# Batch 0 of a Fourier mixing and gated FFN kernel stored in the layout of the other batches

## The chip, the cores and the metric

One of the eight cores of a Trainium2 chip runs the whole program. The metric is the device time of one execution in microseconds (us); the figure before is the median of three runs. A profiled execution stands beside them, and every duration in this text comes from it. A core has TensorE (PE in the profile; its weight loads are PEld), VectorE (DVE), ScalarE (ACT), GpSimd (POOL) and SyncE (SP), which here issues nearly all DMAs. Each engine works through its own instructions in order, and semaphores hold an instruction back until its inputs are there.

## What is computed

```python
def _attn_ref(x):                      # x: (8, 3008, 256) float32
    X = np.fft.fft(x, axis=1)
    X = np.fft.fft(X, axis=2)
    return X.real.astype(np.float32)

def _moe_ref(x, w_gate, w_val, w_out): # x: (24064, 256); 256x1536, 256x1536, 1536x256
    gate = 1.0 / (1.0 + np.exp(-(x @ w_gate)))
    val = x @ w_val
    return (gate * val @ w_out).astype(np.float32)
```

The second function is applied to the first one's result, flattened to 24064 rows. The three weight arrays come as float64 and are converted on the chip.

## The kernel before

**The transform.** S is 3008 rows, M = S/2 = 1504, D = 256. The real part of the transform along the rows needs a cosine sum `pk` of one half of the features and a sine sum `qk` of the other. Rows s, S-s, M+s and M-s are given together as four "h" planes; folding them (additions and subtractions of planes) leaves sums over s = 0..752 for even k and for odd k (`blk` 0 and 1), with the tables `stab` of cosines and sines. The transform along the features is folded too, and its matrix `dt` is multiplied into the gate and value weights beforehand (`merge`, tiles `ps`, copied to `G`). The feature at position D/2 has a row of its own, E, which enters through `ge` and `EK`: `seed` writes E times `ge` into a gate tile's PSUM bank before the products are added to it.

**The loop.** Per batch there are six chunks of k (252 columns, the last 246) and twelve tiles of 128 hidden units, 576 iterations in all. Iteration i does `front_a(i)` (products of `pk` into the PSUM tile `pf`), `gate_a(i-1)` (a sigmoid into h, and z = ae - pf on VectorE), `part(i)` (a ScalarE copy `ae` of the half-finished `pf`, two buffers), `seed(i+1)`, `gate_b(i-1)` (h times pf; a sigmoid; h times z; then sums of h on GpSimd, tile `sf`), `back` (five of fifteen products of a group of three tiles with the output weights, tile `po`, five iterations after the group's first tile) and `front_b(i)` (products of `qk`). Work that is due once stands in a dictionary `side` by iteration. Sums of `po` on VectorE (`c`), transposes and stores wait in the list `later`; two or three are done at the end of each iteration. `NFT`, called `i0` there, is 12. The group of iterations 3p, 3p+1, 3p+2 is called group p.

**Batches 1 to 7** take their x from a DRAM copy `XR` that `mirror_x` lays out: partitions 0 to 63 hold even s, 64 to 127 odd s, and positions 3 to 5 hold the rows 752-s. `fold_ops` folds them on GpSimd, spread over the iterations before; `whole` then does the sums of one `blk` with pairs of matmuls over 63 rows each (`both`). All sums of batch 1 stand in iteration 64 (`g0`); those of a later batch stand 40 iterations into the batch before it. For odd k these batches turn x by tangents on VectorE (`TURN`) and use a table that `table_odd` prepares on GpSimd.

**Batch 0 and the opening.** Batch 0's x and table lie row s = 6p+q on partition p, q in 0..5 (126 partitions), and are loaded in thirds of q. Eight weight tiles of 256 columns (`weight_load`, jobs 0 to 7) come first on SP, then thirds of x and of the cosine table in turn, the sine table, and jobs 8 to 13. A conversion is two ScalarE passes (`weight_parts`), three VectorE passes and one GpSimd addition (`weight_join`); then TensorE merges. `ge_sums` makes `ge` of a merged tile with products of one column. After all eight, VectorE folds the thirds (`third`, `feats`), each followed on TensorE by the E products (`e0_sums`) and the cosine sums of that third (`sums`, 126 rows). `e0_copies`, `e0_row` and `e0_spread` build E's row and its chunk; `then` and `places` combine even and odd sums into `pk`. The sine sums follow, between the first `front_a`. Twelve warming products (`warm`) run before the first weight is there.

E of batches 1 to 7 is folded on GpSimd at iteration 36 (`e_fold`), multiplied at iteration 40 (`e_sums`, 126 rows) and combined on VectorE. At iteration 42 `table_again` loads the table once more, in the other batches' layout. `e_rows` loads a chunk of E's row into `EK`, eleven iterations ahead.

## Time and profile before

| | us |
|---|---|
| median of three runs | 1928.14 (1926.18 to 1929.38) |
| the profiled execution | 1926.51 |
| its span | 1924.7 |
| TensorE busy | 1915.4 |
| VectorE busy | 1430.8 |
| ScalarE busy | 1346.6 |
| GpSimd busy | 1563.8 |

The page divides the span into 40 slices; a digit is the busy share of a slice in tenths. "Busy" for TensorE runs from a matmul's start to a modelled end, so it hides short gaps; starts in the timeline are the surer reading. A float32 matmul appears as two records. In the timeline's lines the columns are the start in us, the length of the run of equal instructions, engine, line, operation, out<-in, shapes and count; in brackets stands the idle time before it and what ended it. A line of the matmuls is always L135, so they are told apart by tile.

Two groups of the table of costliest work are of use beside the lines below: GpSimd's additions of 128 columns by 384 take 1.014 us (L452) and those of 512 columns 1.289 (L436); VectorE's product of 252 columns takes 0.405 (L702).

### The profile page before, as it was taken

The page shows a single profiled execution, that of the slowest core. Times are in us where ns is not written, and L with a number is a line of the kernel's source. Part 1 is how long each engine was busy: PE and PEld are TensorE (multiplying, and loading weights), DVE is VectorE, ACT ScalarE, POOL GpSimd, SP SyncE. Part 2 cuts the span into 40 slices and gives each one's busy share as a digit, 9 for nine tenths or more (in the row PEclk, how much of TensorE's full clock was granted, in tenths as well). Part 3 has the DMA queues.
Part 4 walks back from the last instruction along what each step waited for, and adds up shares of the span by engine and source line. Part 5 has one row for each costly group of instructions (what it writes and reads, how often), then busy time and mean ns, then how long its engine had stood idle before and what let it go on. Part 6 is the DMA issues. An engine that isn't in the chain of part 4 may idle for free.

```text
span 1924.7 us, 34460 instructions
## 1 busy us (share of the span) xinstructions
PE 1915.4 (100%) x11260; PEld 1787.2 (93%) x11260; DVE 1430.8 (74%) x3210; ACT 1346.6 (70%) x3147; POOL 1563.8 (81%) x2806
## 2 busy tenths in 40 slices
PE   9999999999999999999999999999999999999999
PEld 6899989999999999999999999999999999999998
DVE  7747887787777877777777777777777777777776
ACT  5877667767777677776777767777677767777775
POOL 3499989978898788986888878888788986777775
PEclk9999999999999999999999999999999999999999
DMA  9451422211131211202112121121200100011101
GB/s 305 135 87 38 106 80 56 52 58 37 20 76 27 80 17 29 76 14 80 25 46 51 20 81 21 47 50 25 80 14 15 26 17 14 15 22 20 26 17 30
DMA packets 167403, 97.89 MB, mean 51 GB/s; under 512 B 128602, under 2 KB 157372, under 8 KB 165432
## 3 DMA queue, kind: packets, MB, share of 16 engines
q1 hardware_dynamic: 166670, 95.17, 20.6%
q8 instruction: 91, 1.49, 0.3%
q14 instruction: 88, 0.72, 0.1%
q10 hardware_dynamic: 522, 0.50, 0.1%
q0 software_dynamic: 32, 0.00, 0.0%
HBM read 70.40 MB, written 47.24 MB: 61 GB/s over the span
## 4 chain that ended last, share of the span: by engine, by line
PE 94%; DMA 3%; DVE 1%; ACT 0%; SPq 0%; issue 0%; ACTq 0%; DVEq 0%
PE pf L135 49%; PE po L135 40%; PE ev L135 2%; DMA st<-in_stab_dram 2%; PE rows L135 1%; PE od L135 1%; DMA xr<-in_xf_dram 1%; DMA wc<-in_moe_w_gate_dram 1%; DVE c L830 0%; PE row L135 0%; DMA raw<-in_moe_w_val_dram 0%; DVE z L690 0%; PE ps L135 0%; ACT pf L703 0%; DVE h L706 0%
## 5 line engine op out<-in xcount | busy, mean ns | idle before, releaser
L712 POOL TENSOR_TENSOR sf<-h 128x168 f32<-128x168 f32 (+1 forms) x935 | 517.6, 573 | 210.9 <-DVE h L706 210.8
L712 POOL TENSOR_TENSOR sf<-h,sf 128x168 f32<-128x168 f32 (+1 forms) x1122 | 624.5, 577 | 58.2 <-DVE h L706 57.9
L135 PE MATMUL pf<-qk,G 128*128 128x252 f32 (+1 forms) x2304 | 582.7, 376 | 1.2 <-ACT ae L675 1.1
L135 PE MATMUL pf<-pk,G 128*128 128x252 f32 (+1 forms) x2304 | 583.0, 376 | 0.8 <-ACT pf L664 0.8
L706 DVE TENSOR_TENSOR h<-pf,z 128x252 f32<-128x252 f32 (+1 forms) x576 | 241.8, 420 | 425.7 <-ACT pf L703 425.7
L664 ACT ACTIVATE pf<-ek,ge 128x252 f32<-128x252 f32 (+1 forms) x1152 | 542.8, 471 | 19.2 <-DVE h L706 0.2
L135 PE MATMUL po<-sf,wf 128*128 128x168 f32 (+1 forms) x2992 | 516.2, 305 | 0.0
L675 ACT ACTIVATE ae<-pf 128x504 f32<-128x504 f32 (+1 forms) x576 | 339.6, 590 | 233.1 <-PE pf L135 230.4
L135 PEld LDWEIGHTS pf<-pk,G 128*128 128x128 f32 x2304 | 436.3, 190 | 54.5 <-issue 2.3
L135 PEld LDWEIGHTS po<-sf,wf 128*128 128x128 f32 x2992 | 460.6, 190 | 8.0
L135 PE MATMUL po<-h,wf 128*128 128x168 f32 (+1 forms) x2618 | 463.3, 305 | 0.0
L830 DVE TENSOR_TENSOR c<-c 128x168 f32<-128x168 f32 (+1 forms) x929 | 437.9, 503 | 5.0
L135 PEld LDWEIGHTS pf<-qk,G 128*128 128x128 f32 x2304 | 410.6, 190 | 28.8 <-ACT ae L675 2.8
L135 PEld LDWEIGHTS po<-h,wf 128*128 128x128 f32 x2618 | 416.6, 190 | 16.2
L690 DVE TENSOR_TENSOR z<-ae,pf 128x504 f32<-128x504 f32 (+1 forms) x576 | 383.7, 666 | 32.4 <-ACT h L689 31.0
L689 ACT ACTIVATE h<-pf 128x252 f32<-128x252 f32 (+1 forms) x576 | 218.0, 379 | 161.3 <-PE pf L135 157.2
L703 ACT ACTIVATE pf<-z 128x252 f32<-128x252 f32 (+1 forms) x576 | 214.2, 372 | 84.6 <-DVE h L702 81.9
L702 DVE TENSOR_TENSOR h<-h,pf 128x252 f32<-128x252 f32 (+1 forms) x576 | 233.0, 405 | 0.0
L712 POOL TENSOR_TENSOR sf<-sf 128x168 f32<-128x168 f32 (+1 forms) x187 | 108.0, 577 | 14.7
L712 POOL TENSOR_TENSOR sf<-sf,h 128x168 f32<-128x168 f32 (+1 forms) x187 | 102.1, 546 | 0.0
L743 ACT COPY c<-po 128x504 f32<-128x504 f32 (+1 forms) x141 | 80.1, 569 | 0.0
L839 DVE STREAM_TRANSPOSE os<-c 128x256 f32<-128x256 f32 x184 | 70.6, 422 | 0.3 <-issue 0.3
(152 smaller groups left out, 903.4 us busy)
## 6 DMA issues: line engine op xcount, KB each, us to landing
x<-xr SPq DMA_DIRECT2D x14, 1536.0 KB
out_dram<-os SPq DMA_DIRECT2D x368, 56.0 KB
xr<-in_xf_dram SPq DMA_DIRECT2D x14, 768.0 KB
xr<-in_xf_dram SPq DMA_DIRECT2D x35, 256.0 KB
ek<-ed SPq DMA_DIRECT2D x39, 126.0 KB
out_dram<-os SPq DMA_DIRECT2D x284, 7.0 KB
st<-in_stab_dram SPq DMA_DIRECT2D x6, 658.9 KB
x<-in_xf_dram SPq DMA_DIRECT2D x3, 1024.0 KB
```

Of the source, the lines that this page charges most:

```text
L135: nc.tensor.matmul(o, l, r, start=start, stop=stop, skip_group_check=True)
L664: nc.scalar.activation(PF[i][:, g], EK[i // NFT], AF.Copy, scale=ge[:, g, f : f + 1])
L675: nc.scalar.activation(AP[i], PF[i], AF.Copy, scale=2.0)
L689: nc.scalar.activation(H[p][:, fh, 0:n], PF[i][:, 0], AF.Sigmoid)
L690: nc.vector.tensor_tensor(z[:, :, ::-1], AP.pop(i), PF[i], op=ALU.subtract)
L702: nc.vector.tensor_tensor(h[:, fh, 0:n], h[:, fh, 0:n], pf[:, 1], op=ALU.mult)
L703: nc.scalar.activation(pf[:, 0], z[:, 0], AF.Sigmoid)
L706: nc.vector.tensor_tensor(h[:, fh, n:], pf[:, 0], z[:, 1], op=ALU.mult)
L712: nc.gpsimd.tensor_tensor(block(p, dst), block(p, a), block(p, b), op=(ALU.subtract, ALU.add)[op])
L743: (nc.vector.tensor_copy if t == 1 or t == 3 and not last else nc.scalar.copy)(C[0][:, 3 * t * R : 3 * (t + 1) * R], PO[t][:, 0 : 3 * R])
L830: engine.tensor_tensor(t[:, dst * R : (dst + 1) * R], *v, op=(ALU.subtract, ALU.add)[op])
L839: nc.vector.transpose(os_[0][:, s, 0:nb, h, :], t[:, c0 : c0 + nb * TB])
```

## The change

Batch 0 gets the other batches' layout. `half_rows` now puts even s on partitions 64 to 127 and odd s on 0 to 63, for all batches. The rows s of a third come with two DMAs of 64 partitions, the rows 752-s with four more (one for each plane). The table is 128 partitions of three positions, sines and cosines together, loaded once; `table_again` is gone. Even k of batch 0 is folded once more (two additions in `third`) and summed in pairs over 63 rows with half the columns; odd k is summed in three products per position, one of them with features negated on ScalarE (`minus`). `feats` of thirds 0 and 1 runs on GpSimd. E's products are eight (batch 0) or four at a time over half the rows and go through small DMAs (`e_move`) into `EROW`; `e_fill` combines them on GpSimd, at iterations 42 and 54 for batches 1 to 7. In the opening the thirds stand between conversions 5, 6 and 7, weight 0 is converted in halves, `dt` is loaded on SP behind weight 1, and eight warming products remain. In the loop one entry of `later` moves between the two VectorE products of `gate_b`, and conversion 11 moves from iteration 0 to 1.

```diff
...
+    def half_rows(par, q=0, mirror=False):
+        n = HP if mirror is None else HP - 1 - (q == N3 - 1 and (par or mirror))
+        return slice((1 - par) * HP, (1 - par) * HP + n)
     def load_third(j):
+        copy = nc.sync.dma_start
+        for par in range(2):
+            copy(out=X[0][half_rows(par, mirror=None), :, j], in_=xf[0, 0:HP, :, 2 * j + par])
+        first, step = [xf[0, t // NQ, 0, t % NQ].offset for t in (M // 2 - 2 * j - 1, M // 2 - 2 * j)]
+        for h in range(4):
+            src = bass.AP(xf.tensor, first + h * NQ * D, [[step - first, 2], [-4 * NQ * D, HP], [1, D]])
+            copy(out=X[0][:, h, N3 + j], in_=src)
...
-    def table_again():
...
+    def load_table(j):
+        for par in range(2):
+            nc.sync.dma_start(out=ST[0][half_rows(par, mirror=None), :, j], in_=stab[0:HP, :, 2 * j + par])
...
-            def third(q):
+            def third(j):
+                q = slice(j, NQ, N3)
+                tt = nc.vector.tensor_tensor
                 a, m = x4[:, 0:3:2, q], x4[:, 1:4:2, q]
                 tt(a[:, :, :, 0], a[:, :, :, 0], m[:, :, :, 0], op=ALU.add)
                 tt(a[:, :, :, 1:D], a[:, :, :, 1:D], m[:, :, :, D - 1 : 0 : -1], op=ALU.add)
                 across(nc.vector, 0, q)
                 across(nc.vector, 1, q)
-            def feats(q):
-                v, r = x4[:, 0:2, q], x4[:, 2:4, q]
-                nc.vector.memset(r[:, :, :, 0:1], 0.0)
+                if j == N3 - 1:
+                    nc.scalar.copy(x4[P - TB :, 3, q], x4[P - TB :, 1, j].unsqueeze(1).to_broadcast([TB, 2, D]))
+                rows = slice(0, P - 2 if j == N3 - 1 else P)
+                for i, op in enumerate((ALU.add, ALU.subtract)):
+                    tt(x4[rows, 3, i * N3 + j], x4[rows, 1, j], x4[rows, 1, N3 + j], op=op)
+            def feats(j, e):
+                q = slice(j, NQ, N3)
+                v, r = x4[:, 3::-3, q], x4[:, 1:3, q]
+                e.memset(r[:, :, :, 0:1], 0.0)
                 lo, hi = v[:, :, :, 1:HD], v[:, :, :, D - 1 : HD : -1]
-                tt(r[:, :, :, 1:HD], lo, hi, op=ALU.subtract)
-                tt(lo, lo, hi, op=ALU.add)
-            for q in qs:
-                ops += [lambda q=q: third(q), lambda q=q: feats(q)]
+                e.tensor_tensor(r[:, :, :, 1:HD], lo, hi, op=ALU.subtract)
+                e.tensor_tensor(lo, lo, hi, op=ALU.add)
+            def minus(j):
+                for to, of in ((2, 0), (1, 2)):
+                    nc.scalar.mul(x4[:, to, N3 + j, HD:D], x4[:, of, N3 + j, 0:HD], -1.0)
+            ops = third, feats, minus
...
-        def sums(*qs):
-            for q in sorted(qs, key=lambda q: q % 2):
-                mm((ev, od)[q % 2], w(q), ST[0][0:NP, int(sn), q, c0 : c0 + n], q < 2, q >= NQ - 2)
+        def sums(j):
+            halves = [(sum_, half_rows(par, j)) for par, sum_ in enumerate((ev, od))]
+            if not blk:
+                for r in range(2):
+                    for sum_, rows in halves:
+                        mm(sum_[:, r::2], w(j + N3 * (r ^ int(sn)))[rows],
+                           ST[0][rows, int(sn), j, r:NE:2], j == 0 and r == 0, j == N3 - 1)
+                return
+            for sum_, rows in halves:
+                mm(sum_, w(j)[rows], ST[0][rows, int(sn), j, NE:], j == 0, False)
+            halves = [(sum_, half_rows(par, j, True)) for par, sum_ in enumerate((ev, od))]
+            for r in range(2):
+                for sum_, rows in halves:
+                    x_ = WN[int(sn)][:, j] if r else w(N3 + j)
+                    mm(sum_[:, r::2], x_[rows], ST[0][rows, 1 - int(sn), j, NE + r :: 2], False,
+                       j == N3 - 1)
...
+    def e_products(w, m, blk, ps, q, fresh=True):
+        out_ = []
+        for r in range(2):
+            for par in range(2):
+                rows = half_rows(par, q, blk and r)
+                if blk:
+                    g, tab = 1 - par + 2 * r, ST[0][rows, r, q, NE:]
+                else:
+                    g, tab = par + 2 * r, ST[0][rows, 0, q, r : NE + r : 2]
+                out_.append(lambda g=g, rows=rows, tab=tab, r=r: mm(
+                    ps[g * TB : g * TB + m, 0 : tab.shape[-1]], w(q + N3 * r)[rows], tab,
+                    fresh and q == 0, q == N3 - 1))
...
+    def e_move(m, blk):
+        c0, n = ((0, NE - NE // 2), (NE, NO))[blk]
+        for g in range(4):
+            nc.sync.dma_start(out=EROW[0:m, g, c0 : c0 + n], in_=ECOPY[g * TB : g * TB + m, c0 : c0 + n])
+    def e_fill(m, blk):
+        er, tt = shared["er"], nc.gpsimd.tensor_tensor
+        e = EROW[0:m]
+        if blk:
+            e = e[:, :, NE:]
+            for r, op in enumerate((ALU.add, ALU.subtract)):
+                tt(e[:, 0:2, r::2], e[:, 0:2, r::2], e[:, 2:4, r::2], op=op)
+            tt(er[0:m, 1 : 2 * NO : 2], e[:, 1], e[:, 0], op=ALU.add)
+            tt(er[0:m, M - 1 : M - 1 - 2 * NO : -2], e[:, 1], e[:, 0], op=ALU.subtract)
+            return
+        nc.gpsimd.memset(er[0:m, NK:], 0.0)
+        for r in range(2):
+            n, h = NE // 2 + 1 - r, NO // 2
+            ev, od = e[:, 2 * r], e[:, 2 * r + 1]
+            tt(er[0:m, 2 * r : 2 * r + 4 * n - 3 : 4], ev[:, 0:n], od[:, 0:n], op=ALU.add)
+            tt(er[0:m, M - 2 * r : M - 2 * r - 4 * h : -4], ev[:, 0:h], od[:, 0:h], op=ALU.subtract)
...
-        for q in (2 * j, 2 * j + 1):
-            for blk in range(2):
-                c0, n = ((0, NE), (NE, NO))[blk]
-                row = (2 * blk + q % 2) * TB
-                mm(E0["ps"][row : row + 1, 0:n], W[0, blk][2][:, q], ST[0][0:NP, 0, q, c0 : c0 + n],
-                   not j, j == N3 - 1)
...
+            E0["ps"] = [bank("pe", NB - 1), bank("pe")]
+            mm(E0["ps"][1], nil[0:1, 0, 0:P], dt[0:1].rearrange("p t d -> p (t d)"), True, False)
+        some = [e_products(lambda q, blk=blk: W[0, blk][2][:, q], TB, blk, E0["ps"][blk], j, not blk)
+                for blk in range(2)]
+        for a, b in zip(*some):
+            b()
+            a()
...
+        for i, (c0, k0, step) in enumerate(((0, 0, 1), (0, 2, 1), (NE, 1, 2), (NE + 1, 3, 2))):
+            mm(ps[:, k0::4], sel[:, i], ECOPY[:, c0 : c0 + step * (h - 1) + 1 : step],
+               not i, True)
...
+    def e_sums(blk):
         ps = bank("pe", NB - 1)
         m = B - 1
...
+        for q in range(N3):
+            for f in e_products(lambda q: xm[:, q, :, 1] if blk else xs[:, q], m, blk, ps, q):
+                f()
+        e_copy(m, blk, ps)
+        e_move(m, blk)
...
     load_x(0)
-    for j in range(8):
+    weight_load(0)
+    weight_load(1)
+    nc.sync.dma_start(out=dt, in_=dtab.rearrange("(c p) d -> p c d", p=P))
+    for j in range(2, 6):
         weight_load(j)
-    for j in range(N3):
-        load_third(j)
-        load_table(0, j)
+    load_third(0)
+    weight_load(6)
+    load_table(0)
+    load_third(1)
+    weight_load(7)
+    load_third(2)
+    load_table(1)
+    load_table(2)
...
-    warm(12)
+    shared["er"] = pqp.tile([P, NK + 1], F32, name="er", tag="pk")
+    warm(8)
     ges = None
-    for j in range(8):
-        weight_parts(j)
+    for j in range(6):
+        for c in ((slice(0, 1), slice(1, 2)) if not j else (slice(0, 2),)):
+            weight_parts(j, c)
+            weight_join(j, j % 3, c)
         if j > 2:
             merged(j - 3)
-        weight_join(j, j % 3)
         weight_use(j)
-        if j > 2 and j < 7:
+        if j > 2:
             ges = ge_sums((j - 3,), 3, ges)
+    for j in range(8, KEEP):
+        weight_load(j)
+    third, feats, minus = fold_ops(0, 2)
+    third(0)
+    feats(0, nc.gpsimd)
+    merged(3)
+    ge_sums((3,), 3, ges)
     ge_out(range(4), ges)
-    for j in (5, 6, 7):
-        merged(j)
-    for j in range(N3):
-        if j == N3 - 1:
-            weight_load(8)
-            weight_load(9)
-        load_table(1, j)
-    for j in range(10, KEEP):
-        weight_load(j)
     seq_start(0)
-    folds = fold_ops(0, 2)
     cos = [seq_group(0, blk, 0, (2 * blk, 2 * blk + 1)) for blk in range(2)]
-    for j in range(N3):
-        folds[2 * j]()
-        e0_sums(j)
-        folds[2 * j + 1]()
-        if j == N3 - 1:
-            e0_copies()
-            e0_row()
-        for sums, _, _ in cos:
-            sums(2 * j, 2 * j + 1)
-    put = [then() for _, then, _ in cos]
+    weight_parts(6)
+    merged(4)
+    minus(0)
+    weight_join(6, -1)
+    for sums, _, _ in cos:
+        sums(0)
+    weight_use(6)
+    third(1)
+    feats(1, nc.gpsimd)
+    weight_parts(7)
+    merged(5)
+    merged(6)
+    minus(1)
+    weight_join(7, -1)
+    for sums, _, _ in cos:
+        sums(1)
+    weight_use(7)
+    third(2)
+    e0_sums(0)
+    e0_sums(1)
+    feats(2, nc.vector)
+    merged(7)
+    minus(2)
+    e0_sums(2)
+    for blk in range(2):
+        e_copy(1, blk, E0["ps"][blk])
+    put = []
+    for sums, then, _ in cos:
+        sums(2)
+        put.append(then())
     for f in put:
         f()
+    for blk in range(2):
+        e_move(1, blk)
     e0_spread()
     for i in range(N3):
         seed(i)
     for j in (8, 9):
         weight_parts(j)
         weight_join(j, NB - 1)
+    for blk in range(2):
+        e_fill(1, blk)
     sin = [seq_group(0, blk, 1, (2 * blk, 2 * blk + 1)) for blk in range(2)]
     for j in range(N3):
-        sines(j)
-        front_a(j)
-        if j < 2:
-            part(j)
-        if not j:
-            weight_parts(10)
-            weight_join(10, NB - 1)
-    put = [then() for _, then, _ in sin]
-    for high in range(2):
-        for f in put:
-            f(high)
+        sin[0][0](j)
+    front_a(0)
+    part(0)
+    put = [sin[0][1]()]
+    put[0]()
+    sin[1][0](0)
+    front_a(1)
+    part(1)
+    weight_parts(10)
...
-    for j, i in ((11, 0), (12, 3), (13, 5), (14, 6), (15, 8), (16, 10), (17, 12)):
-        if i > 0:
+    for j, i in ((11, 1), (12, 3), (13, 5), (14, 6), (15, 8), (16, 10), (17, 12)):
+        if j > 11:
...
-    at(3 * i0, e_fold)
-    later_e = []
-    at(3 * i0 + 4, lambda: later_e.extend(e_sums()))
-    at(3 * i0 + 5, lambda: later_e[0]())
-    at(3 * i0 + 6, lambda: later_e[1]())
-    at(3 * i0 + 6, table_again)
+    at(2 * i0 + 2, e_fold)
+    at(2 * i0 + 5, e_mirror)
+    at(3 * i0, e_across)
+    for blk in range(2):
+        at((3 + blk) * i0 + 4, lambda blk=blk: e_sums(blk))
+        at((3 + blk) * i0 + 6, lambda blk=blk: e_fill(B - 1, blk))
+    at(4 * i0 + 7, lambda: nc.sync.dma_start(out=ed[1:], in_=shared["er"][0 : B - 1]))
     at(4 * i0 + 5, lambda: [at(4 * i0 + i, f) for i, f in zip((8, 9, 10, 11, 12, 7), table_odd())])
     for i in range(i0, count, i0):
-        at(i - 11, lambda i=i: e_rows(i))
+        at(i - 11 + 3 * (i == i0), lambda i=i: e_rows(i))
...
+        n = 3 if i >= count - 8 else 2 + i % 2 - (3 * i0 + 4 <= i <= 3 * i0 + 6)
         if i:
-            gate_b(i - 1, mid.pop(i, []))
+            between = mid.pop(i, []) if i > 1 else []
+            if not between and later:
+                between = [later.pop(0)]
+                n -= 1
+            gate_b(i - 1, between)
...
```

## The prediction

> **What bounds the kernel now.** I read the page first: the span, the clock row and the chain of waits.
>
> ```profile
> span 1924.7 us, 34460 instructions
> ...
> PEclk9999999999999999999999999999999999999999
> ...
> PE 94%; DMA 3%; DVE 1%; ACT 0%; SPq 0%; issue 0%; ACTq 0%; DVEq 0%
> ```
>
> TensorE carries 94% of the chain at full clock: 576 iterations that begin 3.125 us apart (3.43 in about the first 15, which also merge weights). Only what changes TensorE's work or makes it wait counts. So I looked for places where it is not paced by itself, and found two, both touched: the opening up to about 60 us and the stretch from 231 to 259 us. The profiled execution took 1926.51 us, 1.8 around the span; the median of the runs is 1928.14. My sums are differences from the profiled execution and are added to the median.
>
> The opening, in TensorE's timeline (start, length, instruction):
>
> ```profile
> 15.28 1.99 PE L135 MATMUL ps<-wqk,dt 128*128 128x256 f32 x8
> ...
> 17.73 1.99 PE L135 MATMUL ps<-wqk,dt 128*128 128x256 f32 x8
> ...
> 51.05 1.01 PE L135 MATMUL pf<-qk,G 128*128 128x252 f32 x4
> ...
> 59.53 1.01 PE L135 MATMUL pf<-qk,G 128*128 128x252 f32 x4
> ```
>
> Merges with their small `ge` products come 2.45 us apart, the first second half of a gate tile (`pf<-qk`) starts at 51.05 and that of iteration 3 at 59.53. Between 27 and 38 us TensorE follows VectorE, which works without a gap from 5.25 to 35.33 (eight conversions of 2.1 us, three folds of 4.2). VectorE's timeline shows one more price:
>
> ```profile
> 23.28 2.38 DVE L436 TENSOR_TENSOR x<-x 126x512 f32<-126x512 f32 x2
> ...
> 28.35 1.42 DVE L436 TENSOR_TENSOR x<-x 126x512 f32<-126x512 f32 x2
> ```
>
> The same two additions take 1.42 us alone and 2.38 while GpSimd does its part of conversion 7: 0.96 lost, and that GpSimd part takes 2.24 instead of 1.29. Last, the table by stretch, DMA share and GB/s in its last two columns:
>
> ```profile
> core 0: us, PE busy (x) PEld busy (x) DVE busy (x) ACT busy (x) POOL busy (x), PEclk, DMA share, GB/s
> 4.00:13.00 9.00, 8.64 (x35) 6.68 (x33) 7.39 (x11) 6.66 (x11) 3.72 (x3) 1.00 1.05 390
> 194.00:203.00 9.00, 9.00 (x54) 8.46 (x53) 7.65 (x17) 6.08 (x15) 8.84 (x17) 1.00 1.05 216
> ```
>
> The first stretch loads weights into all 128 partitions; the second reloads the table, 64 partitions at a time. The 16 engines are busy in both, at 390 and 216 GB/s.
>
> The later stretch: GpSimd's timeline, then TensorE's.
>
> ```profile
> 252.04 1.61 POOL L224 TENSOR_SCALAR st<-st 128x561 f32<-128x561 f32 x1
> 253.63 1.54 POOL L712 TENSOR_TENSOR sf<-h,sf 128x168 f32<-128x168 f32 x3
> ...
> 256.44 0.54 POOL L712 TENSOR_TENSOR sf<-sf 128x168 f32<-128x168 f32 x1
> ```
>
> ```profile
> 241.70 1.12 PE L135 MATMUL pf<-qk,G 128*128 128x252 f32 x4 [0.23 <-ACT ae L675]
> ...
> 245.62 1.10 PE L135 MATMUL pf<-qk,G 128*128 128x246 f32 x4 [0.54 <-ACT ae L675]
> ...
> 257.38 1.59 PE L135 MATMUL po<-sf,wf 128*128 128x168 f32 x10
> 258.81 0.99 PE L135 MATMUL pf<-qk,G 128*128 128x246 f32 x4
> ```
>
> Iterations 55 to 63 begin up to 3.92 us apart, 2.6 us too many in all, because VectorE is late (the waits named are on `ae`, which ScalarE can write only after VectorE's z). GpSimd has not been idle since 207.91 and finishes the sums of group 19 at 256.98, 0.4 us before TensorE starts the block that uses them.
>
> **The change, opening.** TensorE's own work falls. Eight warming products instead of twelve: eight records of 0.21 us less, and merge 0 could start at 6.95 instead of 8.89, -1.9. The 24 sums over 126 rows (0.633 each, 15.2) become 11.4: even k in pairs of 0.32 that run side by side, as the later batches' pairs do at 260 us (0.16 us per pair of records), odd k at the old length. E rises from 3x0.73 to one 512-column product (0.86) and 3x0.65, +0.6; should its eight tiles not run together (four did, at 180 us), +2 more. E's four-part spread costs between 0.2 and 0.6; I take 0.2. Sum -4.9, if TensorE set the pace. I find that it does not, and follow the chain.
>
> (a) Weight 0 in halves: 256 KB less at 390 GB/s is 0.66 us earlier, but six half operations of 0.405 (as L702) replace three of 0.7. Conversion 1 begins at 6.8 instead of 7.52, and merges 3 to 5 with `ge` run from 14.6 to 21.95; the fourth `ge` is out 0.64 later (24.56 to 25.20 before), at 22.6.
> (b) ScalarE now copies `ge` ahead of the parts of weight 6, so those and what is queued behind them (the copy of merge 4, the negations of third 0) wait until 22.7. VectorE, done with third 0 near 21 to 22, idles. Conversion 6: 23.4 to 25.5.
> (c) Third 1 on VectorE: 0.08+1.25+1.42 as in the rows L473, L474, L436, two new additions of 256 columns (2x0.405), and 0.96 for GpSimd's part of conversion 6 beside it: 4.5, to 30.0. Bounds: 3.6 without the collision, 5.5 with two.
> (d) Its features move to GpSimd: 2x1.29 (512 columns) for VectorE's 1.37: to 32.6.
> (e) The data. Weights 0 to 5 and `dt` are in at 12.15. A third is half direct rows, which go to 64 partitions (0.524 MB at 216 GB/s, 2.4 us), and half mirrored rows, which go to all 128 (1.35 at 390; 2.4 if they too are slow): 3.8 to 4.9, and I take 3.8, since the weights' loads to all 128 partitions are the nearer row. Its six issues at 0.55 each (the old one's length on SP) take 3.3, less than the data. A table third is 0.77 MB in halves: 3.6. In the order of issue third 1 is in at 24.9, third 2 at 30.1, table 1 at 33.65. So the sums of third 1 start at 33.65; 31.6 would be the start with neither a slow load nor (c)'s collision, 36.8 with slow mirrors.
> The row above is a reload while DRAM copies were queued behind it. [...]
> (f) TensorE: sums 1.9, merge 7 1.73, E 0.86+3x0.65, last sums 1.9: 42.0. VectorE's third 2 (4.5, plus 0.75 for a ScalarE copy in its middle) and features (1.4) end at 38.8, the negations at 39.4, in time.
> (g) Spread 0.6 with latency, its copy 0.38, six seeds 2.78 (row at 39.23), the parts of weight 8 0.67, conversions 8 and 9, the even sine places 1.0, conversion 10, one place 0.5: 0.6+0.4+2.8+0.7+4.2+1.0+2.1+0.5 = 12.3. Iteration 0's `pf<-qk` starts near 54.5, 3.5 late. Conversion 11 moves one iteration later, so iteration 2 waits less: 7.8 to iteration 3 instead of 8.48. The opening costs **+2.8**, between +0.7 (sums at 31.6) and +5.9 (at 36.8).
>
> Covered, at nothing: eight small row copies and the write of E's row on SP. Behind them stand the loads of weights 14 to 17, which wait for the sines until about 50 us anyway, and `ge` and E rows not read before iteration 7; without that cover, 8x0.45 us.
>
> **The change, 125 to 271 us.** E's products for seven batches: before 5.54-3.13 = 2.4 us of TensorE in iteration 40; after 0.95 and 1.9, each with the same 0.5 beside it, 3.85: +1.45. The table reload goes. VectorE's idle 0.45 us between the two h products takes one of the `later` sums, which would return the 2.6 us and 0.4 of the 12.03 between `pf<-qk` at 258.81 and 270.84 (11.64 at later batches). But E's additions, 2.8 us on VectorE before, go to GpSimd: four of 189 columns at iteration 42 (0.54 each between the rows of 168 and 254 columns, 2.2), offset by the fold moved to iteration 26 (1.1 less 0.5) and 1.5 us of GpSimd idle at 204 to 208; and four of 376 at iteration 54 (1.01 each for 384 columns, L452), 4.0, where nothing is idle. They push group 19's sums from 256.98 to 261.0; its last matmul and `pf<-qk` follow 0.4 later, at 261.4 against 258.81. TensorE's extra 1.45 and VectorE's stalls disappear inside this wait. **+2.6-0.4 = +2.2**; +0.8 if seven-partition rows cost 0.65 each, +3.4 at 1.3.
>
> In iterations after 72 `between` and the swapped halves change nothing: VectorE had slack there, and TensorE does the same work. The small copies that mirror E's rows go out on SP at iterations 26 and 29 and are read at 36. The write of E's rows waits on SP for those four additions until about 238; the stores behind it come at 246.
>
> Sum: 2.8+2.2 = **+5.0**, 1931.5 for the profiled execution, **1933.1** for the median. Own range +1.5 to +9.3: 1929.6 to 1937.4.
>
> **Rivals.**
> A, not slower: TensorE paces the opening. Place: the sums of third 1. If folded data and table are there when TensorE ends merge 6 and its first sums (about 29.5), it never waits. The opening gives -4.9, with GpSimd's +2.2 -2.7: 1925.4. For: TensorE waits only 1.9 us in the old opening, and VectorE's own work stays equal (2.4 more of additions, 2.7 less of features). Against: the idle of (b) and the rates of (d) and (e).
> B: GpSimd's additions find cover, iterations 55 to 64 return 3.0 less 1.45: 2.8-1.55, 1929.4. For: group 20 is not needed before 271. Against: no idle since 207.91.
> A and B together: -4.9-1.55, 1921.7.
> C, the clock: TensorE would idle from 29.5 to 33.65. The first records in the trace are 0.42 us apart until 5.5 us, then 0.21; such a restart would cost half of 4.3 us, +2.1: 1935.2. No idle of that length is in the trace. [...]
> That halved work is not done at all I exclude: the shapes follow from the diff.
>
> **Chances.** Forecast 0.47, A 0.12, B 0.12, both 0.16, C 0.13. 0.2% is 3.9 us, about what a measurement here tells from no change. The forecast's +5.0, spread over its range, lies above it two times in three (0.32), C always (0.13), B and A seldom (0.05): slower 0.50. Faster: both (0.15) and part of A (0.05), 0.20. Within: 0.30. The range 1923.5 to 1937.5 leaves out most of "both" and the far tail.
>
> **What would show it.** Right: a TensorE gap of some 4 us before the sums of third 1, waiting for GpSimd or the table; VectorE idle near 21 to 23; `pf<-qk` of iteration 3 at 61 to 63; GpSimd without idle and TensorE waiting for it before `pf<-qk` of iteration 64. Wrong: iteration 3 before 58 us, or iterations 55 to 64 all near 3.1 us apart.

## The result and the profile after

| | before | after |
|---|---|---|
| median of five runs, us | 1928.14 | 1982.28 |
| range | 1926.18 to 1929.43 | 1980.99 to 1984.74 |
| ratio, 95% interval | | 1.0283 (1.0272 to 1.0295) |
| span of the profiled execution | 1924.7 | 1982.6 |
| iteration 3, start of `pf<-qk` | 59.53 | 111.76 |
| from there to iteration 65 | 211.31 | 217.29 |

The change costs 54 us where 5 were predicted. The two spans differ by 57.9, more than the medians, because the profiled execution after is the slowest of its five and the one before is among the fastest. Of the 57.9, 52.2 lie ahead of iteration 3, 6.0 between it and iteration 65, and -0.3 behind. Both places are those that the prediction named; both were priced too low, the first by a factor of more than 18. The page after:

```profile
span 1982.6 us, 34806 instructions
...
PEclk7699999999999999999999999999999999999999
...
PE 94%; SPq 2%; DMA 1%; ACT 1%; DVE 1%; POOL 1%; issue 0%; ACTq 0%; DVEq 0%; POOLq 0%
```

The first two slices of the clock row (49.6 us each) are no longer at 9, and SP's queue has 2% of the chain, some 40 us; before it had none. SP's timeline says what it was doing (start, length, instruction, count):

```profile
7.47 10.81 SPq L165 DMA_DIRECT2D x<-in_xf_dram  x4
18.33 2.67 SPq L304 DMA_DIRECT2D wf<-in_moe_w_gate_dram  x1
...
23.69 15.71 SPq L165 DMA_DIRECT2D x<-in_xf_dram  x4
39.45 2.65 SPq L304 DMA_DIRECT2D wf<-in_moe_w_val_dram  x1
...
43.90 11.85 SPq L165 DMA_DIRECT2D x<-in_xf_dram  x4
55.79 4.61 SPq L221 DMA_DIRECT2D st<-in_stab_dram  x4
```

L165 is the mirrored load of one plane of a third, 128 KB. Four take 10.8 to 15.7 us of SP, and the weight behind them 2.67 instead of 0.47. It is the issues themselves that are long. The DMAs of SP take eight semaphores in turn, so each also waits for the one eight places ahead of it, but those had landed: SP's waits ahead of the mirrored loads come to 0.3 us in all. Several long issues end just as the load three places ahead lands (18.28 and 18.25, 39.40 and 39.40, 58.47 and 58.50). So a slow load holds the issues of the next ones; what sets how many fit into the queue isn't shown. The table by stretch for the changed kernel (clock, DMA share and GB/s last):

```profile
16.00:20.00 4.00, 4.00 (x19) 3.34 (x20) 2.53 (x4) 1.12 (x2) 2.55 (x2) 1.00 0.13 47
38.00:42.00 4.00, 1.03 (x4) 0.00 (x0) 0.00 (x0) 0.00 (x0) 0.00 (x0) 0.50 0.14 47
```

While mirrors load, the 16 DMA engines are 0.13 busy and move 47 GB/s, what two engines would be and move at the rate of the weights' loads (2/16 = 0.125; 390/16 = 24.4 GB/s each). 128 KB at 47 GB/s are 2.8 us. The mirror's source has an outermost dimension of two (the two parities). A row of the kernel before has the same pattern with four. What runs then are copies into DRAM, of which three of 256 KB, issued from 66.7 us on, have the four planes as their outermost dimension; the last of these lands at 79.3:

```profile
78.00:80.00 2.00, 2.00 (x11) 1.76 (x10) 1.97 (x5) 1.39 (x4) 0.96 (x1) 1.00 0.28 99
```

So an outermost dimension of 2 stands beside 0.13 and 47 GB/s, one of 4 beside 0.28 and 99: about as many engines as it has entries, in these two cases.

TensorE's timeline after:

```profile
22.80 1.05 PE L135 MATMUL ge<-busy,G 1*128 1x1 f32 x8
36.08 0.68 PE L135 MATMUL ev<-st,x 63*128 63x189 f32 x1 [12.23 <-POOL x L498]
...
75.19 0.99 PE L135 MATMUL ev<-st,x 63*128 63x188 f32 x2 [36.16 <-DMA wc<-in_moe_w_out_dram]
76.05 0.68 PE L135 MATMUL od<-st,x 63*128 63x188 f32 x1
...
77.60 3.04 PE L135 MATMUL ps<-wf,dt 128*128 128x256 f32 x8
...
102.84 1.12 PE L135 MATMUL pf<-qk,G 128*128 128x252 f32 x4 [0.39 <-DVE qk L571]
```

Two gaps, 12.2 and 36.2 us. The first ends with the features of third 0, whose mirrors are in at 29.8. The second is strange: the sums at 75.19 still belong to third 0, whose x and table have been there since 34.9. The weight named as releaser is no input of theirs. The two loads of the last table land at 75.1 and 76.0, just ahead of the even and the odd sum at 75.19 and 76.05. Merge 6 at 77.60 takes 3.04 instead of 1.99: the granted clock is 0.50 from 25.1 to 79.8 us.

The later stretch, on VectorE, GpSimd and TensorE:

```profile
290.39 0.18 DVE L246 RECIPROCAL odd<-st 128x3 f32<-128x3 f32 x1 [5.24 <-POOL er L628]
```

```profile
286.13 2.24 POOL L626 TENSOR_TENSOR odd<-odd 7x376 f32<-7x376 f32 x2
...
289.39 0.97 POOL L628 TENSOR_TENSOR er<-odd 7x376 f32<-7x376 f32 x1
```

```profile
284.81 1.59 PE L135 MATMUL po<-h,wf 128*128 128x168 f32 x10
...
293.46 1.12 PE L135 MATMUL pf<-qk,G 128*128 128x252 f32 x4 [3.93 <-ACT ae L736]
...
295.75 2.80 PE L135 MATMUL po<-sf,wf 128*128 128x168 f32 x10
```

VectorE is idle 5.24 us in front of the reciprocal of the tangents until GpSimd has done E's additions; TensorE, which gets no `ae` meanwhile, waits 3.93 and then works at a granted clock of 0.50 from 294.8 to 298.2 us (ten products in 2.80 instead of 1.59).

### The profile page after: what moved, and what is told of

Its sections match the earlier page's. It is cut to its first block, busy times and chain, and to the rows that moved or that the text cites. A ratio compares the mean times of both kernels' runs of the same rounds, so it can differ in the third digit from the quotient of the medians.

```text
span 1982.6 us, 34806 instructions
## 1 busy us (share of the span) xinstructions
PE 1918.4 (97%) x11380; PEld 1792.8 (90%) x11380; DVE 1402.0 (71%) x3203; ACT 1345.3 (68%) x3159; POOL 1575.0 (79%) x2842
## 4 chain that ended last, share of the span: by engine, by line
PE 94%; SPq 2%; DMA 1%; ACT 1%; DVE 1%; POOL 1%; issue 0%; ACTq 0%; DVEq 0%; POOLq 0%
PE pf L135 49%; PE po L135 40%; PE ev L135 3%; SPq L165 2%; PE rows L135 1%; DMA st<-in_stab_dram 1%; PE od L135 1%; PE ps L135 0%; SPq L304 0%; PE pe L135 0%; PE row L135 0%; DMA dt<-in_dtab_dram 0%; POOL sf L773 0%; ACT pf L725 0%; DMA wc<-in_moe_w_out_dram 0%
## 5 line engine op out<-in xcount | busy, mean ns | idle before, releaser
L773 POOL TENSOR_TENSOR sf<-h,sf 128x168 f32<-128x168 f32 (+1 forms) x1122 | 613.7, 568 | 48.2 <-DVE h L767 46.8
L891 DVE TENSOR_TENSOR c<-c 128x168 f32<-128x168 f32 (+1 forms) x929 | 426.0, 467 | 3.4
L764 ACT ACTIVATE pf<-z 128x252 f32<-128x252 f32 (+1 forms) x576 | 211.5, 367 | 26.5 <-DVE h L763 23.1
L773 POOL TENSOR_TENSOR sf<-sf 128x168 f32<-128x168 f32 (+1 forms) x187 | 103.5, 553 | 14.7
L773 POOL TENSOR_TENSOR sf<-sf,h 128x168 f32<-128x168 f32 (+1 forms) x187 | 110.1, 589 | 0.0
L135 PE MATMUL ev<-st,x 63*128 63x189 f32 (+3 forms) x228 | 45.7, 348 | 48.4 <-DMA wc<-in_moe_w_out_dram 36.2
L135 PEld LDWEIGHTS ev<-st,x 63*128 63x128 f32 (+1 forms) x228 | 39.2, 190 | 52.5 <-DMA st<-in_stab_dram 37.3
```

The source lines that it names most:

```text
L135: nc.tensor.matmul(o, l, r, start=start, stop=stop, skip_group_check=True)
L764: nc.scalar.activation(pf[:, 0], z[:, 0], AF.Sigmoid)
L773: nc.gpsimd.tensor_tensor(block(p, dst), block(p, a), block(p, b), op=(ALU.subtract, ALU.add)[op])
L891: engine.tensor_tensor(t[:, dst * R : (dst + 1) * R], *v, op=(ALU.subtract, ALU.add)[op])
```

## The experiments

Times are medians beside runs of the kernel before on the same chip; "iteration 3" is the start of `pf<-qk` in the profiled execution, "stretch" the time from there to iteration 65.

| run | us | before | ratio (95%) | iteration 3 | stretch |
|---|---|---|---|---|---|
| e1_rows64 | 1953.98 | 1927.98 | 1.0129 (1.0112 to 1.0146) | 81.48 | 217.7 |
| e2_forward | 1985.12 | 1927.98 | one run | 111.41 | 218.0 |
| e3_tangent | 1983.57 | 1927.98 | 1.0284 (1.0269 to 1.0299) | 110.31 | 217.5 |
| e5_pool | 1962.19 | 1927.98 | one run | 88.81 | 217.5 |
| e4_between | 1927.36 | 1929.03 | 0.9995 (0.9986 to 1.0004) | 63.08 | 210.7 |
| e6_table | 1975.05 | 1929.03 | one run | 102.04 | 217.2 |
| e7_rows64_table | 1947.44 | 1929.03 | 1.0089 (1.0075 to 1.0103) | 73.78 | 217.7 |
| e8_fill | 1943.81 | 1929.03 | 1.0075 (1.0059 to 1.0090) | 73.28 | 214.6 |
| e9_host | 1939.58 | 1927.83 | 1.0056 (1.0041 to 1.0071) | 65.57 | 217.3 |
| e10_host_spread | 1941.42 | 1927.83 | 1.0069 (1.0052 to 1.0085) | 66.66 | 219.1 |
| e13_before_half | 1927.52 | 1928.41 | 0.9992 (0.9984 to 1.0001) | 62.64 | 208.8 |
| e14_best_after | 1935.35 | 1928.41 | 1.0037 (1.0024 to 1.0050) | 66.58 | 212.8 |
| e15_warm | 1933.48 | 1928.69 | 1.0022 (1.0013 to 1.0032) | 67.60 | 212.8 |

### The mirrored loads

e1: four loads a third as before, each over 64 rows of one parity and two planes, rows rising.

```diff
-            src = bass.AP(..., [[step - first, 2], [-4 * NQ * D, HP], [1, D]])
+            src = bass.AP(..., [[4 * NQ * D, HP], [NQ * D, 2], [1, D]])   # per parity, two planes
```

> The mirrored loads of batch 0 in as many transfers of as many bytes (four of 128 KB a third), but each over the 64 rows of one parity, rows in rising order (so the mirrored half of batch 0's x holds the wrong rows). Theory 1, the engines: a transfer whose outermost dimension has two entries is carried by two of the 16 DMA engines (47 GB/s, 2.7 us for 128 KB, as the trace of the changed kernel shows); over 64 rows it is carried by all of them: mirrored loads at about 216 GB/s (0.6 us each), no idle time over 5 us on TensorE before the sums of third 1, which start at 31 to 37 us instead of 75; iteration 0's second half at 54 to 58 instead of 102.8; time 1934 to 1940 us (1928.1, +2.8 to +5.9 in the opening, +6.0 in the stretch to 271 us that this leaves as it is). Theory 2, the reversal of the rows costs the time: this run shows about the same, 1934 to 1940, and the next one too. Theory 3, the count of 1 KB packets or of transfers: no change, 1980 to 1984.

e2: two parities outermost, rows rising (`[4 * NQ * D, HP]`).

> The mirrored loads as in the changed kernel, 128 partitions with an outermost dimension of two, but rows in rising order (wrong rows again). Theory 1, two engines: nothing changes, 2.7 us for each of the twelve, time 1980 to 1985. Theory 2, the reversal: the loads run at 390 GB/s and the time falls to 1931 to 1938. Theory 3, packets or count: nothing changes, as theory 1; the run before tells these two apart.

e5: the same loads as in the changed kernel, on GpSimd's queue (`nc.gpsimd.dma_start`).

> The twelve mirrored loads of the changed kernel, right rows, issued by GpSimd instead of SP, ahead of its conversions. Theory 1 with fixed engines: each runs on the same two engines whoever issues it: 12 x 2.7 = 33 us for them, but SP's queue is free, so weights, direct rows and tables come as predicted (table 1 by about 30 us) and the last mirror is in at about 40 us; iteration 0 at 60 to 66 us, time 1940 to 1948. Theory 1 with engines that change from transfer to transfer: the mirrors spread over the 16 engines and are in by 15 to 25 us; what remains is GpSimd's own time for twelve issues (0.77 us for the one in the trace, 9.2 us in all), which delay conversion 0 from 5.8 to about 15: time 1940 to 1950 too, but with the mirrors in early. If the time stays above 1975, the queue that issues is not what matters and the load's own 2.7 us are.

e2 changes nothing (four mirrors 11.37 us on SP): it isn't the reversal. e1, with the same bytes and packets, takes 28 us off: the outermost dimension is the cause, worth 30.3 us at iteration 3 (111.76 to 81.48). The semaphores agree. A mirrored load of the changed kernel raises its semaphore once right behind its issue and twice on landing, 8 to 14 us later; the copies with four planes outermost raise theirs once and then four times, and the two loads of rows s of third 0, which have 64 rows outermost, sixteen times each on landing (13.26 to 15.16 and 14.49 to 15.92 us). A reversed load over 64 rows wasn't tried. But e1 misses its 1934 to 1940 by 14 us; the stretch table and TensorE's timeline of e1 show why:

```profile
12.00:28.00 16.00, 13.61 (x66) 10.93 (x68) 12.21 (x21) 7.14 (x15) 8.63 (x8) 0.94 1.11 223
```

```profile
43.39 0.99 PE L135 MATMUL ev<-st,x 63*128 63x188 f32 x2 [14.18 <-DMA wf<-in_moe_w_gate_dram]
45.14 0.68 PE L135 MATMUL od<-st,x 63*128 63x188 f32 x1 [0.76 <-DMA st<-in_stab_dram]
```

All engines are now busy, at 223 GB/s, and the odd-k sums of third 0 still wait for the last table (its two loads land at 43.3 and 45.1). e5 frees SP (-20 us), but misses its 1940 to 1950 by 12: GpSimd's last four issues wait for earlier mirrors to land, so its part of conversion 0 starts at 23.2 us instead of 5.8. Which engines carry the mirrors in e5 its rows don't tell, since other loads run beside them.

### The wait for the table

```diff
-    ST = [const.tile([P, 2, N3, NE + NO], F32, name="st"), ...
+    ST = [const.tile([P, N3, 2, NE + NO], F32, name="st").rearrange("p q t k -> p t q k"), ...
```

> The changed kernel with the table's tile laid out third by third, so that a load of one third covers one unbroken stretch of each partition. In the changed kernel the odd sums of third 0, which read the sine half of its table, wait until 75.2 us, though their own table and x are in by 37. Theory 1: they wait for the loads of the later thirds, whose stretch (cosine half to sine half) takes in the sine half of third 0; with the new layout they run by 40 us, and merge 6, the sums of third 1 and merge 7 (1.6, 3.0, 2.2 and 2.0 us) move ahead of the last table: iteration 0's second half near 94 instead of 102.8 us, time 1973. Theory 2: they wait for something else that comes late (weights, x): no change, 1982.

> Both: mirrored loads over 64 rows with rising rows (wrong rows in the mirrored half of batch 0's x) and the table's tile third by third. With the odd sums of third 0 no longer waiting for the last table, TensorE has left only E's products and the sums of third 2 when that table comes, at 44 to 45 us: iteration 0's second half near 63 us instead of 72.5; time 1944.7. If theory 1 on the table is wrong: 1954, as without it.

Theory 1 holds in both, at 1975.05 and 1947.44 for 1973 and 1944.7 (iteration 0 at 93.11 for 94, and at 64.84 for 63). In the changed kernel a load of one third writes its cosines and its sines, with the other thirds' between them, and the program gave the odd-k sums of third 0 (its sines) waits for the loads of thirds 1 and 2. It costs 9.7 us at iteration 3 with the slow mirrors, 7.7 without. In e7's timeline the sums of third 1 then wait for their own table:

```profile
38.07 0.96 PE L135 MATMUL ev<-st,x 63*128 63x189 f32 x2 [4.93 <-DVE x L485]
39.76 0.65 PE L135 MATMUL od<-st,x 63*128 63x189 f32 x1 [0.72 <-DMA st<-in_stab_dram]
```

### Loads that fill 64 partitions

e9 hands over batch 0's x and the table as they lie on the chip, so each load is one block of 128 partitions.

```diff
+        for q in (j, N3 + j):
+            nc.sync.dma_start(out=X[0][:, :, q], in_=xa[:, :, q])
...
+        nc.sync.dma_start(out=ST[0][:, :, j], in_=sta[:, j])
```

> The changed kernel with batch 0's x and the table handed over in the order in which they lie on the chip (two more inputs, each row only moved), so that every load fills all 128 partitions, and the table's tile third by third. Right rows, right result. Theory 1: what is left of the opening's loss after the mirrors and the table's tile is the rate of loads that fill 64 partitions (225 GB/s from 12 to 44 us with the mirrors over 64 rows, weights among them too); at 390 GB/s the data are in by 29 us, VectorE and GpSimd pace third 1 as predicted (sums of third 1 at 31.6 to 32.6), iteration 0's second half is at 53 to 54 and iteration 3's at 62 to 63 (73.8 with half loads): time 1936 to 1938 with the 6.0 us of the later stretch. Theory 2: loads with 1 KB packets are slow whatever the partitions: 1943 to 1948.

Its rates and its sums of third 1:

```profile
12.00:28.00 16.00, 14.00 (x68) 10.96 (x70) 13.79 (x23) 8.63 (x18) 9.43 (x9) 0.92 1.07 386
```

```profile
34.26 0.43 PE L137 MATMUL ev<-st,x 63*128 63x189 f32 x1 [2.67 <-POOL x L492]
```

386 GB/s against 232 in the same stretch of e7, with the same bytes: theory 1, 8.2 us at iteration 3 (73.78 to 65.57). The DMA engines are busy in both (1.07 and 1.11), so the smaller number of issues isn't the reason. Now GpSimd's features pace third 1, as expected. Its time is 1.6 us over the range, and iteration 3 is 2.6 to 3.6 later than expected there.

### The stretch to iteration 65

e3 gives the tangents a tile of their own. e8 and e10 move E's additions; "the run before" is e7 for e8, whose rising rows it keeps, and e9 for e10.

```diff
-    jt, eo, *tans = [extra[:, at_[i] : at_[i + 1]] for i in range(4)]
+    tan = const.tile([P, 2 * N3], F32, name="tan")
```

> The six columns of tangents get a tile of their own instead of lying in the tile where E's rows of the other seven batches are gathered. Theory A: the 5.24 us in which VectorE is idle before its reciprocal (iteration 58, at 290 us) are a wait of that small instruction for GpSimd's additions, which read the place it writes; with its own place that wait goes, and with it TensorE's 4.1 us and the 1.8 us of half clock behind it: time 1982.3 - 5.9 = 1976.4. Theory B, as predicted: GpSimd itself is late by 4 us and TensorE waits for its sums a few iterations later: the wait moves to iterations 60 to 64 and 2 to 4 us stay: 1978 to 1981. Theory C, TensorE's wait has another cause: 1980 to 1985.

> As the run before, and the additions of E's rows for the other seven batches go from GpSimd to VectorE (four of 189 columns and four of 376). Theory A: GpSimd is the bound of the stretch from iteration 52 to 64, and its 4.2 us of additions are what made it 5.8 us longer there (it was so with the wait of the tangents and without it): the stretch gets 3 to 4 us shorter, time 1941. Theory B: TensorE's stop of 3.0 us for the second half of E's products, which leaves GpSimd and VectorE without work, is what costs: at most 1 us shorter, 1944. Theory C: VectorE, which has had little slack there, becomes the bound: 1944 to 1947.

> As the run before, and E's rows of the other seven batches added on VectorE, the four additions of 376 columns one in each of iterations 55 to 58 instead of together in iteration 54 (where the four together made iterations 54 and 55 longer by 2.3 us). Theory A, the stretch to iteration 64 is bound by what is put on GpSimd and in one burst on VectorE: it comes out at 212 to 213 us from iteration 3 to 64 against 211.3 before, 214.6 with the burst and 217.3 in the changed kernel; time 1932 to 1934. Theory B, the products of E themselves in two blocks (4.8 us against 2.4) are all of the rest: 214 to 215 us, time 1935 to 1936.

e3: VectorE's wait is gone and nothing is gained (the stretch is 217.5 us for 217.3). TensorE now waits for GpSimd two and more iterations later:

```profile
298.24 1.05 PE L135 MATMUL po<-sf,wf 128*128 128x168 f32 x4 [1.35 <-POOL sf L775]
```

Iterations 59, 62 and 63 are 1.8, 2.3 and 1.7 us too long in place of 56 and 57. The time, 1983.57, lies in theory C's range, but the place is theory B's: the reciprocal was only the first to wait for a late GpSimd, and all of the loss stays instead of 2 to 4 us. e8 takes the additions off GpSimd and the stretch falls from 217.7 to 214.6, as theory A says (its 1941 us was set beside the 1944.7 expected of e7, which took 1947.44). Of these 3.1 us 2.6 are iteration 57, which runs at half clock in e7 (5.86 us; its four products of `pk` take 1.89) and not in e8 (3.25; they take 1.04), so most of the gain comes by way of the clock. e10 is no test of its theories: spread to iteration 58, the additions wait for GpSimd, which prepares the table of odd k in the same tile (it also overwrites part of E's rows, so E of batches 1 to 7 is lost for odd k there):

```profile
256.49 0.87 DVE L622 TENSOR_TENSOR er<-odd 7x376 f32<-7x376 f32 x1 [4.26 <-POOL odd L223]
```

The halvings of the later batches' table move from GpSimd to ScalarE in e13 and e14:

```diff
-            pool.tensor_scalar(out=j4[...], in0=j4[...], scalar1=0.5, scalar2=None, op0=ALU.mult)
+            nc.scalar.mul(j4[...], j4[...], 0.5)
```

e4 is the kernel before with `between` alone, e13 that and the halvings above on ScalarE; e14 is the changed kernel with all repairs.

> The kernel before with one part of the change alone: in each iteration with no conversion between VectorE's two h products, one of the queued sums is done there. As predicted, this returns the 2.6 us that iterations 55 to 63 begin too far apart and 0.4 of the 12.03 behind them: 1925.1 us against 1928.1, a ratio of 0.9985. Rival: GpSimd, whose sums of group 19 end 0.4 us before TensorE uses them, takes over as the bound: at most 0.4 us are gained, ratio 0.9998. A third: the queued sums now run ahead of an h product that is needed, and the steady iterations get longer: ratio over 1.001.

> The kernel before with VectorE's queued sums between its two h products (as in the run with that part alone) and the two halvings of the later batches' table (1.61 us each on GpSimd) on ScalarE, two iterations later. If GpSimd is the bound of the stretch from 231 to 259 us once VectorE's stalls are gone (TensorE waited 1.8 us for it in one iteration there), 3.2 us less on GpSimd take that wait away: iteration 3 to 65 takes 208.5 to 209.5 us (211.3 before, 210.7 with the sums alone), time 1925.5 to 1926.5 against 1928.1, ratio 0.9985 to 0.9992. Rival: ScalarE, which waits for GpSimd's additions before it can halve, holds up the activations behind it: 211 us or more, ratio over 1.0.

> The changed kernel with all that was found: x of batch 0 and the table handed over in the order in which they lie on the chip, the table's tile third by third, E's rows of the other batches added on VectorE in two parts (iterations 54 and 55), the halvings on ScalarE, and the small table dt loaded from ScalarE's queue, as in the kernel before, instead of behind weight 1 on SP. Opening: if the 1 KB pieces of dt in SP's queue (199 to 285 GB/s from 5 to 7 us against 390 to 406 before) are why conversion 1 began at 8.5 us instead of the predicted 6.8, it begins at 6.8 to 7.2 and iteration 3 comes at 64 instead of 65.6 (59.5 before); if not, at 65.5. Stretch from iteration 3 to 64: 212 to 213.5 (217.3 in the changed kernel, 214.6 with the additions in one burst on VectorE). Time 1933 to 1935.5: still slower than the kernel before, since the chain through VectorE and GpSimd paces the opening.

e4: the rival. VectorE's stalls go, and iteration 62 becomes 4.95 us long instead, waiting for GpSimd:

```profile
257.75 1.05 PE L135 MATMUL po<-sf,wf 128*128 128x168 f32 x4 [1.38 <-POOL sf L712]
```

The stretch gains 0.6 us by this profile; the times, with an interval of 0.9986 to 1.0004, barely tell the rival from the forecast. e13 takes the work off GpSimd, and the stretch falls to 208.8, as expected; its time, 1927.52 for 1925.5 to 1926.5, doesn't follow all the way. It is 0.9 us under the kernel before, with an interval that ends at 1.0001: the nearest to a version that beats both, not shown to be one. e14's time and stretch are as expected; its opening isn't: iteration 3 comes 1.0 later than in e9. Moving `dt` off SP's queue shows no effect: conversion 1 begins at 7.99 in e14 and 8.28 in e15, and in the changed kernel and its nine variants with `dt` on SP anywhere from 7.28 (e2) to 8.49 (e9). e14 starts the sums of third 1 half a microsecond ahead of e9 (33.76 and 34.26) and merge 7 behind them a full one later (37.56 and 36.55): the sums take 3.8 us in e14 and 2.2 in e9.

### The clock

In e14 these sums run at half clock (0.50 granted from 34.0 to 37.4 us). e15 adds five and six warming products in e14's two gaps.

```diff
     ge_out(range(4), ges)
+    warm(5)
...
     weight_use(6)
+    warm(6)
```

> The run before (all that was found) with eleven more warming products in the opening, five before the sums of third 0 and six before those of third 1, where TensorE is idle for 2 to 4 us (0.42 us each at full clock: 2.1 and 2.5 us). Theory 1: the idle time lets the granted clock fall to half for a few us, and where that falls on the sums it costs what they take longer (3.8 instead of 2.2 us for third 1 in the run before): the clock stays at 1.0 between 22 and 48 us, the sums of third 1 take 2.2 us, iteration 0's second half comes near 55.7 instead of 57.65, time 1933.4 against 1935.35. Theory 2: the sums are slow because an input is late: they stay at 3.8 us and the time at 1935; if the products get in the way, 1936.

The stretch tables of e14 and then e15, where third 1 is summed:

```profile
34.00:36.00 2.00, 2.00 (x12) 1.67 (x12) 1.97 (x2) 0.25 (x2) 2.00 (x1) 0.50 1.04 382
36.00:38.00 2.00, 2.00 (x12) 1.39 (x9) 1.96 (x4) 0.61 (x1) 0.00 (x1) 0.64 0.25 87
```

```profile
34.00:36.00 2.00, 2.00 (x11) 1.58 (x9) 1.93 (x4) 0.23 (x1) 1.92 (x2) 1.00 1.04 382
36.00:38.00 2.00, 1.87 (x17) 1.46 (x18) 1.97 (x3) 0.51 (x2) 2.00 (x2) 1.00 0.38 140
...
12.00:18.00 6.00, 6.00 (x14) 4.79 (x15) 5.53 (x9) 2.79 (x5) 3.83 (x3) 0.50 1.06 396
```

The clock holds, the sums of third 1 take 2.2 us instead of 3.8, and the median falls by 1.9 to 1933.48. The two were run on different chips and the intervals of their ratios overlap (1.0024 to 1.0050 and 1.0013 to 1.0032), so the 1.9 is less sure than the 1.6 of the sums. The profiled execution of e15 is the slowest of its ten (1935.90): there the clock fell at 11.2 us instead, in a gap of 2.62 us ahead of merge 1, so its iteration 3 doesn't show the gain.

## Why the prediction was wrong

The direction and the two places were right, and so was the chain through VectorE and GpSimd, once loads no longer hid it (e9). The step that failed is **(e)**, in three of its terms. Iteration 3 splits by the runs into 59.53 before, +6.0 (chain at full loads, e9), +8.2 (64-partition loads and the clock beside them, 0.64 in the mean from 28 to 40 us, e7), +7.7 (the table's wait, e1) and +30.3 (two engines).

- "Half mirrored rows, which go to all 128 (1.35 at 390; 2.4 if they too are slow)". They took 10.8 to 15.7 us of SP a third. Both bounds came from rows whose outermost dimension is 64 or 128; the row with four (78 to 80 us) was in the trace and wasn't looked for. The two rates taken from the table, 216 GB/s for 64 partitions and 390 for 128, bear on the halves (232 in e7, 386 in e9), not on this. "Its six issues at 0.55 each" missed that a slow load holds the issues behind it (2.67 us and more).
- "Sums of third 1 start" when table 1 is in. Nothing was said of which loads the sums of third 0 wait for; they waited for table 2.
- Weights 6 and 7 at 390 GB/s. With half loads in the queue everything ran at 223 to 236 GB/s (e1, e7); with mirrors at 64 rows the data of third 1 were complete at 39.8 us (e7), 3 us past the upper bound of 36.8.
- **(a)** fell: conversion 1 begins at 8.17, not 6.8 (7.52 before). ScalarE can start on weight 1 at 7.48 instead of 6.80; in each microsecond from 3 to 8 the loads run at 199 to 340 GB/s instead of 371 to 406. The cause stays open: with `dt` off SP's queue (e14, e15) conversion 1 begins at 7.99 and 8.28, inside the scatter of 7.28 to 8.49 among the runs with it.
- **(b), (c), (d)** held in e9, all 1.6 us late from (a), which is 8.49 there: VectorE idle from 23.1 to 25.0, third 1 from 27.10 to 31.4 (4.3 for 4.5, the pair of additions 2.39 in collision as priced), features 2.66 for 2.6.
- **(f), (g)**: in e9 9.5 for 8.35 (sums 2.2 for 1.9 us a third, E's products 3.1 for 2.8) and 12.9 for 12.3 (whose end, from 42.0, is 54.3, not 54.5); from iteration 0 to 3 8.93 us instead of 7.8, since conversion 11, moved to iteration 1, held up its own `pf`. With full loads the opening cost 6.0. That this is the prediction's upper bound of 5.9 is luck: that bound is for slow mirrors, and with all data early the prediction's own chain, sums at 32.6 as in (d), gives 1.75. Against the openings of e4 and e13 (63.08 and 62.64) the 6.0 would be 2.5 and 2.9; the medians of e9 and the kernel before, 11.75 apart with 5.95 of it in the stretch, speak for about 6.
- **The stretch**: +6.0 for +2.2, the mechanism right and three terms off. E's products cost 4.8 us instead of 3.85: ScalarE's four copies (1.93 us) stand ahead of the activations, 3.1 us in iterations 52 and 53. And "TensorE's extra 1.45 ... disappear inside this wait" is false: iterations 52 and 53 lose their 3.1 us, and 56 and 57 lose 5.9 on top. While TensorE is held, GpSimd gets no h and is idle as well (0.72 us at 278); what else makes the two add up wasn't separated. A half clock is 1.8 of the 5.9 (iteration 57 at 4.93 instead of 3.12, with 0.50 granted from 294.8 to 298.2 us). That VectorE would wait first, through a shared tile, wasn't seen.
- **Rivals**: C happened, on top of the forecast, not instead; priced +2.1, measured 1.9 by the medians of e14 and e15 (1.6 in the sums of third 1). That idle time brings half clock was a guess there: in the kernel before the clock row is at 9 throughout. The runs showed 0.50 for 3.4 us, in a gap of 1.70 us (e9) and behind one of 2.67 (e14), and in the changed kernel itself from 25.1 to 79.8 us. A and B didn't: TensorE waits even at full loads, and GpSimd's additions found no cover.

## What to carry to other kernels

Before pricing a load by bytes, look at the outermost dimension of its source's pattern (here two entries went with 0.13 of the engines and 47 GB/s, four with 0.28 and 99): the share of busy DMA engines in a stretch where it runs alone shows how many carry it. A tile filled in parts should be laid out so that each load covers an unbroken piece, or later readers wait for loads that they don't need (9.7 and 7.7 us here). A wait that is removed comes back at the next consumer if the engine waited for is late by its amount of work; take work off that engine instead (e3 against e8, e4 against e13).

## What was not expected of the hardware

- Whole 128-partition weights queued between half loads didn't get the 390 GB/s of the kernel before: in e7 the stretch from 12 to 28 us has 232 GB/s and each 2 us from 22 to 42 has 224 to 255, those of weights 6 and 7 among them, and 391 and 386 follow when only whole weights are left (44 to 48).
- In or behind gaps of 1.7 to 2.7 us the granted clock fell to 0.50, for 3.4 us or twice that: in e9 in a gap of 1.70 ahead of third 0 (25.6 to 29.0 us), in e14 behind a gap of 2.67 on third 1 (34.0 to 37.4), in e15's profile in one of 2.62, on merges 1 and 2 (11.2 to 18.0, 6.8 us). It stayed at 1.00 in e14's gap of 1.71 ahead of third 0 and in e9's of 2.67 ahead of third 1, so the length of a gap alone doesn't settle it; what does isn't shown. The change also takes four of the twelve warming products from the start; what that alone does to the clock there wasn't tried.
- The opening of the kernel before isn't the same in each execution: in e4 and e13, which leave it as it is, iteration 3 comes at 63.08 and 62.64 instead of 59.53 (in e4 the third x load lands 0.75 us late or more, in e13 the pairs of sums from 48.15 to 51.78 take 1.33 to 1.46 us instead of about 0.80), and its runs spread from 1926.1 to 1932.1. A term of 3 us in such an opening can't be checked on one profile.
